# Batch 1's two score groups in joint runs of small matmuls, under a redrawn order of all instructions

## The chip, the cores and the metric

One core of one Trainium2 chip runs the whole kernel. The metric is device time in microseconds (us), the median of three runs. The kernel before took 650.4 us (650.25 to 650.64).

## The reference

A bidirectional attention between 512 tokens `x` and 32 state rows `state` (8 batches, 8 heads, depth 64) feeds a gated two-layer network on all 4,352 rows:

```python
scores = scale * x @ state.T;   xread = softmax(scores) @ state     # tokens read states
scores2 = scale * state @ x.T;  sread = softmax(scores2) @ x        # states read tokens
x = concat([xread, sread]) per batch, heads side by side            # (8*544, 512)
out = (x @ w_a) * (x @ w_b) @ w_out                                 # 512 -> 1536 -> 512, float32
```

## The kernel before, in words

The program is recorded first and emitted later. `attn_moe` calls the engines through `rec`, a recorder; each call becomes a *unit*, and `rec.together()` packs several calls of one engine into one unit that stays in one piece. The 4,904 units are numbered in the order of recording. The string `ORDER` then lists all the numbers in the order in which they are emitted. Each engine works through its own units strictly in that order, so `ORDER` fixes for every engine what stands behind what. Waits between engines follow from the data, and from the reuse of buffers. All DMAs are issued by one queue, SP, also in order; eight DMAs can be under way, and the ninth waits for the first of them to land.

The large products (`layer1`, `layer2`, `term`) are float32r matmuls of 128x128 weights on 512 columns, three for each exact product. Batches 0 and 1 (`WIDE`) get their attention from `Attention`, in two groups `g` of four heads each: `load` (DMA of the tokens `x` and states `st`), `scores` (four small float32 matmuls into a PSUM tile), `scores_t` (ScalarE copies the scores to `kept`, four small matmuls turn them), `soft_t`, `exp`, `norm` (softmax on VectorE and ScalarE), `back_t` (four small matmuls turn the result back; ScalarE copies it as `at_h`, a matmul with `neg` takes that off, ScalarE copies the rest as `at_l`). For batch 0 some more small matmuls that nobody reads stand in the same units (`UNREAD`).

Group 0's `load` writes the tile `x_raw`, of which there is one buffer. For batch 1 its DMA therefore waits until batch 0's group 0 has been read for the last time. Batch 0's readers are its scores and `direct0(f)` for f = 0 and 1: `products` of the states with the freshly joined weights `p_raw` (four conversions from 64-bit numbers, each with a DMA `raw<-wl`, an ACTIVATE `t<-raw`, and two VectorE steps). Group 1's `load` has its own tiles, `xg`.

Units that matter below, as numbered before: batch 0's scores 38 and 52, turns 40 and 54, turn back 48 and 62, `direct0` products 14 and 31, their `neg` matmuls 16, 19, 33, 36; batch 1's loads 112 (`x_raw`) and 127, 128 (`xg`), its scores 113 and 129, turns 115 and 131, turns back 123 and 139; batch 0's first-layer matmuls 80 to 91.

TensorE's units in the order before: 38, 40, 52, 54, 14, 16, 19, 48, 50, 80, 31, 62, 81, 129, 64, 82, 33, 36, 83 and so on, with 131 as 26th, 113 as 33rd, 115 as 39th unit. SP's: 6 (`x_raw` of batch 0), 12 (`xg`), 1 (`raw<-wl`), 13 (`xg`, states), 7, 26, 21 (`raw<-wl`), 66 (`raw<-w_out`), 128, 127, 73, 307, 210, 112.

Of the kernel before, what the change touches and what calls it, by code (L numbers as in the profile page):

```python
# [9 lines left out]
F32 = mybir.dt.float32  # L10
# [9 lines left out]
P = 128  # L20
TOK = S + NS
NG = 2
# [120 lines left out]
6 12 1 13 7 0 26 38-39 21 66 40 128 41-42 3 43 2 44 4 52 45 53 127 9 73 8 46 10 54 14-15 307 55 16 27 56 47 28 18  # L143
57-58 29 19 210 48 59 20 22 49 17 50 23 60 67 80 24 51 61 31 538 62 81 63 32 112 68-69 129 35 64 82 33 65 130 36 83 75
143 546 84 86 74 87 230 562 70 88 76 85 71 89 131 90 92 91 212 96 93 220 34 97-99 113 77 37 94 114 102 172 103 132 175
169 78 231 115 176 95 104 100 133 116 144 105 547 106 177 539 101 134 117 211 118 135-136 173 384 225 119 174 107-108
215 145 109 170 120 166 146 121 137 167 171 122 147 168 110 202 206-207 148 198 194 700 123 195 199 149 308 385 221
138 554 111 124 222 226 386 139 156 125 217 213 140 203 208 710 150 126 379 216 227 196 141 151 157 152 218 555 153
158-159 142 394 540 160 154 197 223 161 556 155 228 244 162-163 711 237 200 178-179 541 245 180 712 181 209 395 182
246 387 396 184 542 247 185 183 186-187 190 374 248 239 188 381 713 204 557 397 249 715 189 389 250 309 191 251 164  # L150
274 720 252 268 380 275 253 205 165 382 254 232 391 558 701 312 269 376 313 255 271 261 256-257 571 375 258-259 277
260 401 278 262 272 377 279 703 280 548 233 201 265 283 730 310 281 549 572 284 273 192 282 390 285 299 392 276 286
193 287 311 543 289 234 288 544 408 300 314 290 302 266 315 722 270 316 706 320 398 317 409 411 235 318 412 321 263
717 322 267 410 264 570 319 323 721 326 402 303 403 714 301 324-325 72 723 612 296 573 5 297 348 327 298 293 342 349
224 79 732 399 350 404 574 343 725 656 559 716 344 351 576 238 352 345 740 346 353 575 616 291 595 294 579 240 593 347
333 354 295 731 545 536 355 304 594 241 563-564 330 419 334 339 420 336 577 560 565 421 335 413 362 578 25 422 242 423
414 393 415 724 596 328 598 292 416 356 340 417-418 424 469 341 733 718 337 614 425 370 338 366 597 735 585 832 441
426 657 470 472 371 331 442 363 332 566 443-444 736 586 604 364 737 550 358 445 726 447 599 471 448-449 365 446 605
587 359-360 741 606 361 615 367 702 567 473 450 617 429 368 451 357 453 329 742 435 430 805 369 372 436 568 734 452
437 842 438-439 719 480 637 440 638-639 618 373 620 431 642 607 432 405 454 481 588 427 463 752 482 466 483 753 306  # L160
474 467 484 727 236 589 640-641 608 475-476 433 621 428 643 477 468 478-479 750 434 457 486 672 458 751 460 464 743
# [5 lines left out]
632 1207 1269 674 1259 524 1260 813 633 1261 525 814 1211 1243 760 1244 1218 1267 1245-1246 1202 761 924 1208 1247 652  # L167
1262 634 1212 1248 635 653 758 553 774 1264 1213 1209 1219 1203 1276 1204 535 388 1226 680 1210 914 775 1250 378 675
776 1448 1214 759 654 764 1222 1383 1270 636 777 1277 676 655 762 517 1418 1271 659 833 765 1272 815 1273 1278 1274
709 763 1279 1275 1227 790 1220 1280 660 1281 771 1282 1284 661 678 1215 662 581 834-835 1285 1283 1223 791 1298 1286  # L170
1290 824 915 1287 677 823 666 1288 1291 1289 1228 1221 1292-1293 219 1294 569 825 1299 1301 1296 1300 1295 1302 1450
1297 687 667 1303 827 663 534 1304 1224 1216 770 780 772 1305 781 773 1309 843 829 1306-1307 1229 778 1217 1310 837
779 1311 830 1312-1314 1308 1331 1315 1385 836 817 1317-1318 664 1332 1316 681 1319-1320 1390 826 1225 1334 1321-1322
1329 1323 682 1324 944 1325-1326 831 844 828 1453 1327 1488 668 1335 1328 1342 816 1451 1333 1330 845 1343 1387 665
1449 1344 1336-1337 1364 793 838 819 1338 582 1339 683 839 1386 1340 1345 1341 820 1230 1452 1346-1347 1388 1348
1350-1352 686 1353-1354 1367 840 1231 1349 1356 792 684 1357 1511 1408 1355 818 1368 1365 788 1358-1360 1362 789 1366
846 1389 926 854 782 821 1361 1454 669 855 1391 916 1363 1369 1470 786 925 1409 688-689 847 1393 1370 927 670 783 1394
935 695 1407 917 936 1371 1395 787 1392 1372 1396 601 1397 852 784 1410 685 1398 1373-1374 853 785 1405 679 690 1417
# [12 lines left out]
1553 1602 1596 1609 1555 1592-1593 1613 1002 888 1603 1617 1558 1621 1604 889 1703 1654 950-951 1160 1635 1605 952
1606 1623 810 1607 1559 1655 981 1608 1610 1636 964-965 903 1614 1556 1004 1618 1161 1641 1619 1009 1696 1637 898 1003
# [3 lines left out]
1784 1694 1722 1658 1661 1168 1684 1669 1664-1665 1700 1666 1686 1689 1755 990 1701 1714 1670 1174 976 1671 1708 1985  # L196
1715 1169 912 1170 1690 1899 1006 1013 1705 1764 1709 1702 1691 1716 1697-1698 1710 1672 1667 1164 1175 1717 1711-1713
1747 1723 1668 1718 1728 1795 1720 1749 1699 1719 1752 1732 1748 1753 1840 1733 1721 1734 1171 1738 1767 1750 1739
1729 1014 1785 1765 1735 1751 1007 1740 1754 1736 1182 1724 1758 1757 1741 1759 1737 1742 1766 906 1783 1988 1761 1744
# [161 lines left out]
def attn_moe(ctx, tc, xt, xn, sd, wl, w_out, out):  # L361
# [238 lines left out]
    class Attention:  # L600
# [29 lines left out]
        def unread(self, k, ps):  # L630
            for _ in range(UNREAD.get((self.b, self.g), (0, 0))[k]):
                nc.tensor.transpose(ps[:, :P], ident, ident)

        def scores_t(self, psp, tag):

            sc = self.raw
# [698 lines left out]
```

## Time and profile before

| | us |
|---|---|
| three timed runs, median | 650.4 |
| the profiled execution, own time | 649.11 |
| its span, first to last instruction | 647.3 |
| TensorE busy | 634.6 (98%) |
| VectorE busy | 560.1 (87%) |
| ScalarE busy | 406.6 (63%) |
| mean granted TensorE clock | 0.995 |

PE is TensorE, DVE VectorE, ACT ScalarE; SPq is the DMA issuing queue. Matmul durations overlap, since matmuls are pipelined: what one costs is the distance from its start to the next start. All units show line 1292, where the recorder emits them; so instructions are told apart by tiles (out<-in).

### The profile page before, as it was taken

The numbers are of one execution on the slowest core, as the hardware profiler recorded it, in microseconds if no ns is written. First come the engines' busy times: TensorE is split into PE (matmuls) and PEld (weight loads), VectorE is DVE, ScalarE is ACT, GpSimd is POOL, SyncE is SP. The second block draws the span as 40 slices with busy tenths as digits, with TensorE's granted clock in tenths as the row PEclk, the third lists the DMA queues.
The fourth block names the chain that finished last, engine by engine and source line by source line (L and its number), as shares of the span: only waits on it lengthen the run. The fifth ranks groups of instructions, "written<-read, shape, count | busy, mean of one in ns | idle before, by whom it ended". The sixth has DMA issues, their size and how long they took to land.

```text
span 647.3 us, 10348 instructions
## 1 busy us (share of the span) xinstructions
PE 634.6 (98%) x3554; PEld 496.5 (77%) x3554; DVE 560.1 (87%) x1037; ACT 406.6 (63%) x753; POOL 0.7 (0%) x6
## 2 busy tenths in 40 slices
PE   7999999999999999999999999999999999999996
PEld 4566777768787888787877877878778888888885
DVE  4899999989779999999999999999967886467885
ACT  4698878699896667557658656743643644345331
POOL 0000000000000000000000000000000000000000
PEclk9899999999999999999999999999999999999999
DMA  8897899999999989999799889998887578658516
GB/s 305 292 379 273 276 328 307 301 359 300 299 322 323 327 311 304 319 329 299 251 283 307 280 314 319 308 286 264 286 228 205 170 173 252 210 154 248 158 34 162
DMA packets 145380, 175.54 MB, mean 271 GB/s; under 512 B 48048, under 2 KB 102832, under 8 KB 145328
## 3 DMA queue, kind: packets, MB, share of 16 engines
q1 hardware_dynamic: 145328, 174.89, 83.4%
q8 instruction: 28, 0.46, 0.3%
q14 instruction: 24, 0.20, 0.1%
HBM read 119.80 MB, written 55.05 MB: 270 GB/s over the span
## 4 chain that ended last, share of the span: by engine, by line
PE 88%; DVE 4%; DMA 3%; ACT 3%; issue 2%; SPq 0%; DVEq 0%; ACTq 0%
PE ab L1292 43%; PE acc L1292 34%; PE ms L1292 11%; DMA xg<-xt 1%; DMA x_in<-f_dram 1%; DVE kept_g L1292 1%; DVE p_l L1292 1%; DMA wt<-wo_dram 1%; ACT p_h L1292 1%; ACT wq L1292 1%; SPq L1292 0%; DMA scr<-sw 0%; DVE p_raw L1292 0%; DVE m L1292 0%; DVE xst L1292 0%
## 5 line engine op out<-in xcount | busy, mean ns | idle before, releaser
L1292 PE MATMUL acc<-g_h,wt 128*128 128x512 f32 x588 | 204.0, 392 | 0.0
L1292 ACT COPY a_sb<-ab 128x512 f32<-128x512 f32 (+1 forms) x120 | 67.8, 566 | 146.3 <-PE ab L1292 131.4
L1292 PE MATMUL ab<-at_h,p_h 128*128 128x512 f32 x384 | 148.1, 396 | 1.7 <-DVE kept_g L1292 1.5
L1292 PE MATMUL ab<-at_l,p_h 128*128 128x512 f32 x384 | 146.3, 392 | 0.0
L1292 PE MATMUL ab<-at_h,p_l 128*128 128x512 f32 x384 | 144.7, 392 | 0.7 <-DVE kept_g L1292 0.6
L1292 PEld LDWEIGHTS acc<-g_h,wt 128*128 128x128 f32 x588 | 109.7, 188 | 25.5 <-issue 1.7
L1292 PE MATMUL acc<-g_l,wt 128*128 128x512 f32 x294 | 108.0, 392 | 0.0
L1292 PEld LDWEIGHTS ab<-at_h,p_h 128*128 128x128 f32 x384 | 72.2, 188 | 25.0 <-ACT a_sb L1292 4.8
L1292 DVE TENSOR_TENSOR g_l<-kept_g,g_h 128x512 fp32r<-128x512 f32 x126 | 84.7, 682 | 5.1 <-PE acc L1292 2.7
L1292 PEld LDWEIGHTS ab<-at_h,p_l 128*128 128x128 f32 x384 | 72.1, 188 | 18.7 <-issue 2.5
L1292 ACT CAST g_h<-kept_g 128x512 fp32r<-128x512 f32 x126 | 75.8, 621 | 16.8 <-DVE kept_g L1292 8.3
L1292 PEld LDWEIGHTS ab<-at_l,p_h 128*128 128x128 f32 x384 | 72.3, 188 | 16.0 <-issue 1.2
L1292 DVE TENSOR_TENSOR kept_g<-ab,a_sb 128x512 f32<-128x512 f32 x84 | 57.5, 685 | 30.8 <-PE ab L1292 17.1
L1292 PEld LDWEIGHTS acc<-g_l,wt 128*128 128x128 f32 x294 | 55.1, 188 | 12.2 <-issue 0.8
L1292 DVE TENSOR_TENSOR stg<-acc,stg 128x512 f32<-128x512 f32 x82 | 55.2, 681 | 8.0 <-PE acc L1292 7.2
L1292 PE MATMUL ab<-xs,sw_st 128*128 128x512 f32 (+1 forms) x192 | 51.4, 338 | 0.5 <-DVE kept_g L1292 0.5
L1292 DVE TENSOR_TENSOR p_l<-p_raw,p_h 128x512 fp32r<-128x512 f32 x72 | 48.7, 681 | 2.0 <-issue 1.8
L1292 ACT CAST p_h<-p_raw 128x512 fp32r<-128x512 f32 x72 | 43.4, 621 | 6.1 <-DMA p_raw<-scr 3.7
L1292 ACT COPY sw<-ms 128x512 f32<-128x512 f32 x72 | 41.7, 586 | 8.8 <-PE ms L1292 8.1
L1292 PEld LDWEIGHTS ab<-xs,sw_st 128*128 128x128 f32 x192 | 34.4, 188 | 7.6 <-DVE kept_g L1292 1.2
L1292 PE MATMUL acc<-g_h,wo 128*128 128x512 f32 x96 | 34.0, 398 | 0.0
L1292 DVE TENSOR_TENSOR kept_g<-kept_g 128x512 f32<-128x512 f32 x42 | 28.6, 680 | 0.1
(128 smaller groups left out, 818.0 us busy)
## 6 DMA issues: line engine op xcount, KB each, us to landing
wt<-s_dram SPq DMA_DIRECT2D x42, 512.0 KB, 6.4
scr<-sw SPq DMA_DIRECT2D x72, 256.0 KB, 5.4
p_raw<-scr SPq DMA_DIRECT2D x36, 512.0 KB, 5.9
wt<-wo_dram SPq DMA_DIRECT2D x63, 256.0 KB, 5.0
raw<-wl SPq DMA_DIRECT2D x24, 512.0 KB, 7.9
x_in<-f_dram SPq DMA_DIRECT2D x36, 256.0 KB, 4.8
out<-turned SPq DMA_DIRECT2D x64, 128.0 KB, 4.4
xn<-xn SPq DMA_DIRECT2D x16, 512.0 KB, 5.9
```

The source lines that it names most:

```text
L1292: getattr(obj, method)(*map(real, args), **{k: real(x) for k, x in kw.items()})
```

## The change

For batch 1, `attend` now loads both groups first, then records both groups' four score matmuls as one unit, both groups' four turns as one unit, and both turns back as one unit. The methods are cut apart for it; batch 0 goes the old way. The unit count falls from 4,904 to 4,901, so every number after the place shifts, and `ORDER` is new from end to end:

```diff
 ORDER = """
-6 12 1 13 7 0 26 38-39 21 66 40 128 41-42 3 43 2 44 4 52 45 53 127 9 73 8 46 10 54 14-15 307 55 16 27 56 47 28 18
-57-58 29 19 210 48 59 20 22 49 17 50 23 60 67 80 24 51 61 31 538 62 81 63 32 112 68-69 129 35 64 82 33 65 130 36 83 75
...
+6 38-39 1 7 12 40-41 2 13 42 9 43-44 3 45-46 21 4 8 47 52-53 10 26 54 48 14 23 0 22 49 24 18 55 28 56 27 29 57 66 15
+31 73 50 58 68 113 19 112 32 59 114 80 60 33 51 61 16 81 67 75 62 17 63 35 82 115 74 116 535 64 117 381 536 83 65 34
...
+        def keep(self):
+            nc.scalar.copy(out=self.raw, in_=self.s)
+            self.s = self.raw
+
         def scores_t(self, psp, tag):
...
+            self.keep()
+            self.turn_in(psp, tag)
+            self.turned()
+
+        def turn_in(self, psp, tag):
             self.t = psp.tile([P, 512], F32, name=tag)
             self.sp = half([P, 16, 32], F32, "s_p")
+
+        def turned(self):
             with rec.together():
                 self.unread(1, self.t)
                 for sb in range(4):
...
+                    nc.tensor.transpose(self.t[:, sb * P:(sb + 1) * P], self.s[:, sb * P:(sb + 1) * P], ident)
...
         def back_t(self, psp, tag):
-            ps = psp.tile([P, 512], F32, name=tag)
+            self.turn_back(psp, tag)
+            self.split()
...
+        elif b:
+            gs = [atts[b, g] for g in range(NG)]
+            for a in gs:
+                a.load()
+            with rec.together():
+                for a in gs:
+                    a.scores(*ms)
+            for a in gs:
+                a.keep()
+            for a in gs:
+                a.turn_in(*ms)
+            with rec.together():
+                for a in gs:
+                    a.turned()
+            for a in gs:
+                a.soft_t()
+                a.exp()
+                a.norm()
+            with rec.together():
+                for a in gs:
+                    a.turn_back(*ms)
+            for a in gs:
+                a.split()
+            return
```

In the numbers of before, the new order of TensorE's units begins: 38, 40, 52, 54, 48, 14, 31, 50, 19, 80, 33, 16, 81, 62, 82, then the joint scores (113 with 129), 64, 83, the joint turns (115 with 131), 36, 86, 87, 84, 85 and so on, with the joint turn back as 45th unit. SP's begins: 6 (`x_raw`), 1 and 7 (`raw<-wl`), 12 and 13 (`xg`), 21 and 26 (`raw<-wl`), 66, 73 (`raw<-w_out`), 127 (`xg` of batch 1), 112 (`x_raw` of batch 1), 128 (`xg`, states, of batch 1). The last ten units or so of TensorE are as before but for small swaps. ScalarE's order begins 39, 2, 43, 8, 53, 0, 22, 49, 18, 27, 57, 15, 32, 51, where 2, 8, 22, 27 are the four conversions, 18, 15, 32 copies of the `direct0` products, and 49, 51 the copies behind batch 0's turn back. VectorE's has the four joins 4, 10, 24, 29 as its 8th, 10th, 12th and 16th units.

## Rows read from the trace of the kernel before

**Rows 1.** The page: each engine's busy time and share of the span.

```profile
PE 634.6 (98%) x3554; PEld 496.5 (77%) x3554; DVE 560.1 (87%) x1037; ACT 406.6 (63%) x753; POOL 0.7 (0%) x6
```

**Rows 2.** Stages (us from the span's start): PE busy, granted clock, DMA share, GB/s.

```profile
20.27:40.00 19.73, 19.73 (x132) 1.00 1.00 362
40.00:640.00 600.00, 597.03 (x3319) 1.00 0.84 270
```

**Rows 3.** Whom TensorE waited for, whole span: us in total, times, longest.

```profile
PE ab L1292 <- DVE kept_g L1292: 2.6, 4, 0.8
PE ab L1292 <- DMA xg<-xt: 1.7, 1, 1.7
```

**Rows 4.** SP's timeline: start, duration, instruction of two loads.

```profile
1.93 0.59 SPq L1292 DMA_DIRECT2D raw<-wl  x1
...
19.11 0.34 SPq L1292 DMA_DIRECT2D x_raw<-xt  x1
```

**Rows 5.** What SP waited for between 11 and 20 us.

```profile
SPq L1292 <- PE acc L1292: 6.5, 1, 6.5
```

**Rows 6.** Loads issued at 1.21, 1.93, 0.74 and 19.11: KB, us to landing.

```profile
xg<-xt SPq DMA_DIRECT2D x1, 512.0 KB, 7.4
raw<-wl SPq DMA_DIRECT2D x1, 512.0 KB, 7.9
x_raw<-xt SPq DMA_DIRECT2D x1, 576.0 KB, 3.5
x_raw<-xt SPq DMA_DIRECT2D x1, 576.0 KB, 4.5
```

**Rows 7.** Timeline, 10 to 19 us, PE, ACT and DVE (wait in brackets).

```profile
10.23 1.06 PE L1292 MATMUL ab<-xg 128*32 128x512 f32 x8 [1.73 <-DMA xg<-xt]
...
11.99 0.66 PE L1292 MATMUL ab<-ident,kept 128*128 128x128 f32 x4
...
13.28 0.37 ACT L1292 CAST p_h<-acc 128x256 fp32r<-128x256 f32 x1 [0.76 <-PE acc L1292]
...
13.30 0.64 PE L1292 MATMUL acc<-p_raw,xg 64*32 64x256 f32 x8
...
13.55 0.67 ACT L1292 ACTIVATE t<-raw 128x512 f32<-128x512 f32 x1
...
17.22 0.69 DVE L1292 SCALAR_TENSOR_TENSOR p_raw<-t,t 128x512 int32<-128x512 int32 x1
...
18.42 0.65 PE L1292 MATMUL acc<-p_raw,xg 64*32 64x256 f32 x4
```

**Rows 8.** Timeline of TensorE around batch 1's scores and turns.

```profile
20.27 1.07 PE L1292 MATMUL ms<-xg 128*32 128x512 f32 x8
21.27 0.50 PE L1292 MATMUL ab<-at_h,neg 128*128 128x512 f32 x1
21.61 0.39 PE L1292 MATMUL ab<-at_h,p_l 128*128 128x512 f32 x1
...
23.94 0.60 PE L1292 MATMUL ms<-ident,kept 128*128 128x128 f32 x4
24.30 0.48 PE L1292 MATMUL ab<-at_l,p_h 128*128 128x512 f32 x1
24.61 0.40 PE L1292 MATMUL ab<-at_h,p_l 128*128 128x512 f32 x1
24.84 0.40 PE L1292 MATMUL ab<-at_h,p_h 128*128 128x512 f32 x1
...
25.86 1.07 PE L1292 MATMUL ms<-x_raw 128*32 128x512 f32 x8
```

**Rows 9.** TensorE in three early stretches: length, busy, granted clock, DMA share.

```profile
8.50:10.20 1.70, 0.00 (x0) 1.00 1.05 413
13.20:16.57 3.37, 1.98 (x17) 1.00 1.06 404
16.57:19.98 3.41, 3.24 (x23) 0.50 0.34 125
```

More of the change, by code (lines that the diff above doesn't have):

```diff
@@ L148 @@
[L148 to L157, printed above, removed]
@@ new lines @@
+2158 2326 2307 2512 2396 2328 2553 2444 1052 2354 2261 2493 2397 2171 2355 2400 2338 2308 2339 2343 2584 1071-1072
+2344 2340 2309 2341 1078 2356 2342 2401 2486 2263 2190 1115 2304 2345 2403 2346 2654 2357 2349 2347 2407 2652
+2416-2417 2404 2348 2440 2402 2374 1069 2408 2418-2419 2577 1082 2358 2350 2305 2188 2360 2376 2436 1091 2441 2405
+2422 2420-2421 2423 2588 2448 1092 2375 2409 2424 2410 2437-2438 2428 2425 2474 2426 1089 2427 2377 2635 2191 2439
+2379 2462 2179 1090 2359 1083 1095 2591 2366 2406 2487 2578 2488 2442 2490 2463 2450 2464 2451 2378 2260 1093 2429
@@ new lines @@
+1084 2491 2579 1102 2367 2456 2492 2494 1957 2465 2262 2181 2496 2385 2449 2470 2386 2517 2513 2489 2534 2514-2515
+2368 2387 2457 2556 2554 2369 1096 2453 2388 2518 2572 2454 2519 2452 2471 2458 2389 2370 2516 1081 2455 1099
+2459-2460 2466 2495 2180 2182 1094 2475 2371 2461 2536 2372 2467 2477 2390 1097 2478 2481-2482 2380 2373 2468 2540
+2585 2391 2498-2499 2469 2361 2500 2504 2392 2140 1109 2505-2506 2544 2507 2501-2502 2586 2541 2159 2497 2535 2476
+2503 2580 2537 2508 2510 2542 2576 2509 599 2581 2511 2520 2538 2521 2483 2522 2433 2523 2543 2526 2545 1110 2524 2527
@@ new lines @@
+2682 2747 2803 2740 2804 2772 2794 2815 2807 2721 2773 1149 2161 2805 2808-2809 1130 2806 2810 2818 2880 2594
+2811-2812 2798 2748 2683 2813 2816 2939 2774 2382 2365 2814 1103 2970 2842 2782 2744 2848 2757 2839 1139 2743 2849
+2775 2783 3039 2843-2845 1108 2846 2784 2850 2742 2841 2776 2684 2795 2851 2827 2847 1140-1141 2741 2785 2957 2854
+1129 2861 2858 2864 2796-2797 2865 2819 2940 2143 2866 2852-2853 2928 2867 2859 2799 2862 2971 2868 1131 2759 2800
+2855 2961 2879 1142 2958 1143 2753 2820 3175 2943 2821 1144 2869 2760 3012 1147 2860 2944 2863 2876 2870-2871 2745
@@ new lines @@
+2685 2872 2822-2823 1138 2925 2960 2972 2922 2926 2973 3080 2873 2824 3183 2945 1148 3013 2941 2927 2874 2975 2923
+1132 2875 2829 2777 2946-2947 2162 2934 2924 2942 2833 2962 3020 3072 2755 2877 2948 2983 2930 2830 1145 2834 2383
+2828 2984 2955 3100 2949 2835 2997 2935 2929 2985-2986 3176 2836 2963 3081 2936 2831 2950 2937 2951 3134 2967 2931
+3017 2987 2968 3021 2969 2980 2676 1154 2988 3083 1146 2832 2932 2952-2953 3018 2976 2954 3019 2959 2761 3135 2253
+2964 3022 3040 2144 2995 2956 2933 3014 3025 2965 2767 2989 2768 3026 2163 3073 1152 2762 2769 3015 3044 3082 3191
@@ new lines @@
+2990 2966 3016 3243 3001 2991 3000 2998 2766 2992 3002 2764-2765 3045-3046 2993 2384 3023 2763 2981 2977-2978 2881
+2994 3041 3061 1153 3042 3084 3003 3024 2882-2883 2996 3027-3028 3043 2982 1151 2979 3194 3029-3030 1156 3037
+3008-3009 3067 3235 3133 3031-3032 2901 3047 3033 3062 3048 2884 3313 2903-2904 2902 3068 3314 3034-3035 3049 3036
+2887-2888 3010 3004 2906 3005 3050 3071 3136 3006 2905 3038 3101 3063 3053 3051 2912 3064 3099 1150 3137 3052 3011
+2889 3278 2885 2890 3054 2999 3108 3069 3077 3055 3065 3059 1155 3078 3070 3158 3085 3066 3180 3007 3086 3346 3181
@@ new lines @@
+2907 2913 3056-3057 3087 3074 3139 3184 3088 3058 3210 3089 3236 3079 2914 3090 3182 3060 3075 3177 3211 3091 3076
+3092 3105 3097 2915 3281 3093 3102 3289 2908-2909 3192 3109 3119 3277 2891 3178 3120 3106 3094-3095 3121 3096 3272
+3188 3122 3179 3103 3123 2916 3185 3107 3140 2886 2910 3284 3124 3285 3098 3376 3193 3196 3195 3357 3189 3156 3197
+3131 3311 3186 3464 3104 3190 3252 3198 3216 3125 3157 3126 3187 3127 3688 3271 3110 2786 3128-3129 3234 3301 3276
+3217 3130 3199 3111 3200 3218 3212 3255 3201 3138 3132 3219 2892 3141 3213 2893 3220 3335 3208 3312 3221 3214 3202
@@ new lines @@
+3337 3215 3315 3273 3115 2894 3416 3116 3203 3112-3113 3222 3204 3114 3316 3318 3244 3117 3237 3205 3465 3360 3206
+3358 3238 3223 3207 3253 3148 3256 3118 3209 3319 2895 3317 3240 3320 3241 3161 3254 3300 3242 3257 2917 3142 2896
+3224 3245 3302 3225 3162 3258 2911 3342 3437 3290 3435 3338 3249 3259 2918 3232 3377 3143 3260 2897 3239 3149 3144
+3261-3262 3226-3227 3481 3228-3229 3343 3163 3269 3398 3246 3250 3230 3417 3263 3282 3145 3286 3345 3159 3441 3264
+3160 3150 3231 3265 3233 3283 3266 3339 3344 3251 3267 3438 3307 3579 3359 3308 3247-3248 3321 3268 3440 3340 3322
@@ new lines @@
+3288 3270 2898 3336 3323 3167 3341 3419 3309 3327 3303 3164 3324 3347 3469 3353 3325-3326 3151 3333 3304 3328 3274
+3361 3329 3466 3454 3330 3168 3305 3310 3331 3443 2899 3275 3354 3348 3332 3477 3334 3349 3306 3362 3152 3363 3381
+3364 3368 3365 3478 3366 3369 3146 2919 3406 3367 3165 3554 3382 3370-3371 3383 3279 3374 3384 3372-3373 3280 3407
+3378 3375 3153 3385 3350 3386 3399 3403 3355 3387 3351 3388 3379 3504 3390 3442 3287 3468 3169 3147 3391 3389 3392
+3482 3166 3393 3470 3444 3380 3291 3396 3394 3352 3404 3395 2900 3421 3677 3527 3405 3170 3412-3413 3400 3446 3356
@@ new lines @@
+3418 3397 3580 3427 3422 3428 3297 3450 3423 3429 3447 3519 3295 3689 3467 3420 3171 3298 3430 3401 3296 3471 3414
+3783 3424 3528 3425-3426 3474 3431 3436 3530 3507 3433 3605 3475 3402 3445 3529 3505 3476 3490-3491 3432 3480 3472
+3492 3408 3473 3434 3415 3483 3520 3748 3172 3624 3409-3410 3496 3714 3531 3497 3411 3484 3493-3494 3448 3625 3495
+3439 3524-3525 3449 3453 3173 3452 3451 3685 3498-3499 3508 3485 3509 3455 3293 3500 3502 3501 3154 3606 3526 3532
+3576 3800 3581 3155 3533 3459 3616 3486 3911 3487 3503 3299 3555 3722 3910 2779 3534 3559 3627 3843 3462 3488 3457
@@ new lines @@
+3521 3878 3174 3461 3538 3522-3523 3626 3539 3463 3535 3686 3292 3560 3536 3540 3537 3460 3541 3458 3548 3803 3479
+3489 3544 3556 3561 3615 3456 3876 3617 3611 3877 3557 3515 3577 3643 3542 3801 3558 3562 3510 3563 3653 3543 3552
+3652 3628 3516-3517 3294 3564 3612 3565 3511 3566 3545 3512-3513 3549 3578 3568 3607 3569 3644 3567 2679 3514
+3546-3547 3613 3550 3570 3792 3574 3608 3971 3678 3518 3571 3582 3572 2781 3583 3573 3584 3575 3621 3553 3622 3585
+3551 3900 3645 3609 3590 2790 2778 3618-3619 3586-3587 3623 3782 3620 2787 3591 3588-3589 3592 3614 3682 3649 3598
@@ new lines @@
+3650 3646-3647 3593-3594 3879 3595 3725 3629 3600 3687 3596-3597 3723 3610 3654 3630 2780 3631 3683 3651 3599 3791
+3632 3601 3648 3690 3684 3506 3679 3635 2788 3655 3741 3633 3680 3634 3636 3641 3637 3749 3840 3638 3602 3639-3640
+3922 3715 3656 3659 3663 3719 2251 3664-3666 3642 3669 4017 3667 2678 3668 3660 3670 3675 3720 3784 3671 3681 4036
+3661 3657-3658 3844 3716 3603 3717 3672 3721 3673 3718 3804 3699 3793 2686 3674 3750 3676 3759 4018 3700 3760 3701
+3691 3702 3692-3695 3742 3901 3726 3751 3696-3698 3703 3819 3704-3705 3724 3707 3785 3706 3662 3708 3710 3727 3761
@@ new lines @@
+4352 3728 3963 3709 3729 4020 3730 3974 3731-3733 3941 3734 3711 3745 3735 3788 3752 3739 3762 3768 3712 3736 3786
+2677 3925 3753 3902 3769 3787 2789 3737 3802 3820 3770 2252 3738 3771 3740 3772 3604 3773 3789-3790 3780 2689 3880
+3805 4037 3806 3774-3775 3807 3794 3923 2254 3776-3779 3883 3869 3821 3808 3743 3845 3809 3841 3781 3881 3795 3811
+3842 3796 3810 3812 4214 3817 3884 3813-3815 4355 3816 3797 3854-3855 3798-3799 3882 3856 3972 2688 3857-3858 3818
+3885 3859 3924 4353 4195 3822 4094 3846 4356 3860 3912 3861 3847 3903 3913 2680 4049 3763 3848 3863 3746 3849 3823
@@ new lines @@
+3850-3851 3865 3852 3904-3906 3754 3853 3892 3831-3832 3893 3862 4052 3907 3824 3886 3825 3887 3747 4040 4128 4041
+3894-3895 4039 3896 3888 3864 3908 3889-3890 3909 3891 4095 4196 3744 3870 3898 3942 3975 3918 3873 4476 3949 4038
+4344 3833 3897 3943 3950 4042 3951 3899 3874 3914 4120 3927 3866 3755 3928 3952 3929 3926 3930 3919 4050 3915
+3953-3954 3961 3713 3834 3931-3932 3944 3920 3871 4198 3933 3946 3875 3939 3934 4154 3955 3964 3973 3935-3936 4186
+3956 3937 4053 3957 3947 3958 4197 3959 3945 4021 4155 3976 3948 3968 3938 4080 3965 3960 3921 3940 3962 3916 4007
@@ new lines @@
+4309 4351 4398 4348 4299 4381 4321 4645 4267 4400 4325 4310-4312 4322 4150 4505 4317 4391 4521 4313-4314 4335
+4315-4316 4417 4318 4336 4247 4337-4338 4550 4339 4392 4428 4418 4340 4790 4399 4264 4358 4342 3757 4394 4478 4393
+4359-4361 4323 4811 4362 4366-4367 4419 4363 4395 4569 4368 4326 4268 4369 4503 4249 4584 4364 4453 4370 4614 4581
+4365 4401 4420 4371 4374 4372 4396 4327 4373 4375 4573 4376 3839 4408-4409 4265 4475 4423 4377 4410 4402 4266
+4403-4404 4324 4405 4411 4406-4407 4412 4250 4424 4328 4434 4269 4425 4413 4585 3826 4414 4437 4506 4431-4432 4415
@@ new lines @@
+3829 4435-4436 4443-4444 4454 4438 4812 4433 4439 4455 4426 4382 4440 4456 4421 4529 4445-4446 4441 4378 4442 4457
+4447 4422 4448 4533 4449 4716 4251 4458 4479-4481 4586 4463 4465 4385 4530 4840 4623 4482 4504 4459 4450 4466 4483
+4487 4574 4610 4386 4531 4534 4484-4485 4532 4488-4489 4634 4490 4460 4552 4535 4491 4736 4572 4486 4673 4555 4737
+4553 4492 3828 4495 4556 4493 4551 4582 4379 4611 4676 4494 4557 4507-4508 4469 3758 4509-4511 4558 4497 4496 4464
+4564 4876 4498 4554 4470 4613 4513 4471 4512 4383 4583 4467 4384 4565 4646 4519 4559-4560 4542 4514 4561 4468
@@ new lines @@
+4757 4767 4770 4758 4762 4846 4803-4804 4785-4786 4831-4832 4847 4608 4848-4849 4793 4701 3827 4805 4794-4795 4627
+4834 4609 4850 4836 4854 4759 4628 4855 4835 4702 4769 4698 4703 4806 4851 4760 4810 4629 4870 4699 4852 4837 4796
+4856 4797 4807 4853 4857 4862 4858 4761 4704 4864 4859-4860 4809 4861 4838 4768 4705 4863 4865 4800 4706 4801 4839
+4866 4871 4799 4872 4771 4877 4873 4878 4874-4875 4879 4867 4884 4808 4885 4868 4886-4887 4798 4880 4889 4881 4888
+4882 4896 4891 4897 4890 4892 4898-4899 4893-4894 4900 4895
@@ L632, in unread @@
                 nc.tensor.transpose(ps[:, :P], ident, ident)
+        def keep(self):
+            nc.scalar.copy(out=self.raw, in_=self.s)
+            self.s = self.raw
         def scores_t(self, psp, tag):
-            sc = self.raw
-            nc.scalar.copy(out=sc, in_=self.s)
-            self.s = sc
+            self.keep()
+            self.turn_in(psp, tag)
+            self.turned()
+        def turn_in(self, psp, tag):
             self.t = psp.tile([P, 512], F32, name=tag)
             self.sp = half([P, 16, 32], F32, "s_p")
+        def turned(self):
             with rec.together():
@@ L654, in back_t, with turn_back @@
         def back_t(self, psp, tag):
-            ps = psp.tile([P, 512], F32, name=tag)
+            self.turn_back(psp, tag)
+            self.split()
+        def turn_back(self, psp, tag):
+            ps = self.ps = psp.tile([P, 512], F32, name=tag)
             sp = self.sp.rearrange("p a b -> p (a b)")
@@ L660, in back_t, with split @@
                                      is_transpose=True, start=(sb == 0), stop=(sb == 3))
-            parts_of(ps, *(t[:, self.g, :] for t in a_t[self.b]))
+        def split(self):
+            parts_of(self.ps, *(t[:, self.g, :] for t in a_t[self.b]))
         def soft(self):
@@ L1001, in attend @@
             if b in WIDE:
-                if b:
-                    a.load()
                 where = ms if b or not g else ab
```

287 lines of the change are left out of this document (111 added, 176 removed), and 22 rows, old and new, of the table ORDER.

## The prediction

> **What bounds the kernel now.** I read the share of busy time first: TensorE is busy 98% of the span [rows 1]. A mean can hide stages, so next the stages: from 20.27 us on TensorE has no idle time up to 40, and 2.97 us in the 600 after that [rows 2]. So from 20.27 us on the kernel is one unbroken string of matmuls, and its end is that start plus the matmuls left plus the few waits. The list of waits says which they are: 2.6 us in four waits for `kept_g`, all after 20 us, and 1.7 us for a load, ahead of 20 us [rows 3]. Everything that this change does is therefore judged by two questions: when does the unbroken string start, and how much work is left then? The DMAs are at full share between 20 and 40 us and at 84% later [rows 2], yet TensorE hardly waits for one, so they stay behind it.
>
> The profiled execution took 649.11 us, 1.8 more than its span, and the three timed runs have a median of 650.4. I work out a difference on the profiled execution and put it on the median.
>
> **What the joint runs save on TensorE.** A group's four score matmuls take 1.00 us from start to start (20.27 to 21.27), and the large matmul after them 0.34 (21.27 to 21.61), where a large matmul among its like takes 0.23 (24.61 to 24.84) [rows 8]: the way out of a small run costs 0.1. The second group's run starts from another large matmul at 25.86 and pays this again [rows 8]. One run of eight pays it once, and drains once; I put the gain at 0.3 us, between 0.1 (the way out alone) and 0.5. The four turns take 0.36 (23.94 to 24.30) and their follower 0.31 [rows 8], together 0.67, and the follower alone would have had 0.23: four turns cost 0.44, or 0.11 each. In a run of four or of eight that is the same, so turns and turns back save nothing; bounds 0 and 0.1 each.
>
> **What the joint runs need.** One score unit now needs both groups' loads. Group 0's load, `x_raw`, has one buffer: in the old order SP sat 6.5 us before it, until the `direct0` products of batch 0 had read it [rows 5], and issued it at 19.11 [rows 4]. It was 4.5 us on its way [rows 6], landing at 23.6. That did not matter: group 1, from other tiles, ran at 20.27, and group 0's scores came only at 25.86 [rows 8]. In the new order the joint scores are TensorE's 16th unit, with nothing of length ahead of them after the products. So the landing of `x_raw` sets the start of the unbroken string. I follow the chain to it.
>
> *The loads.* The old order loaded `xg` second; the new one loads two `raw<-wl` first and `xg` fourth. The second load lands at 1.21 + 7.4 = 8.6, the third at 1.93 + 7.9 = 9.8 [rows 4, 6], so a load of 512 KB lands every 1.2 us. The fourth, now `xg`, lands at 11.0, its 64 KB of states at 11.2. Batch 0's second scores start at 11.3 instead of 10.23 [rows 7]. The two last `raw<-wl` land at 12.4 and 13.6.
>
> *The products.* From scores to turns it was 11.99 - 10.23 = 1.76 us [rows 7], so turns now at 13.1, and 0.5 later the turn back of group 0, which the new order puts ahead of the products: 13.6 to 14.1. The first products take some 0.6 and end (with a last duration of 0.4) at 15.0 (one group: 0.64) [rows 7]. ScalarE's order then has the copy `p_h` (0.37) and only behind it the conversion of the last weights (0.67), VectorE the join (0.69) [rows 7]: 15.0 + 0.4 + 0.7 + 0.7 = 16.8. The last products run from 16.8 to 17.5. In the old order they ended at 18.42 + 0.65 = 19.07 [rows 7]. So `x_raw` is issued at 17.5, 1.6 us earlier than before, with the queues as empty as then.
>
> *The load and the string.* Travelling 4.5 us it lands at 22.0; the first `x_raw` of the kernel needed 3.5 [rows 6], which would be 21.0. I take 4.5, since that load too followed a queue of others. The states of group 1 stand behind it on SP and land some 0.2 later. Until then TensorE has eight short units (50, 19, 80, 33, 16, 81, 62, 82), about 2.0 us with ScalarE's copies between them, done at 19.8. It then idles 2.3 us, and behind the joint scores the whole string waits: 64, 83, the turns, and all the first layer.
>
> *The balance.* The string starts at 22.1, not 20.27: +1.8. By then 33 and 82 are done that were not before, 0.12 and 0.23: -0.35. The joint run: -0.3. Sum **+1.2 us**; with a landing at 21.0 it is +0.1, with products that end 0.5 later (bound: their old end at 19.07 minus 1.0) it is +1.7.
>
> **The clock.** TensorE's clock fell once in the old run: from 16.57 to 19.98 it was granted 0.50, its 1.2 GHz level, after 3.4 us in which TensorE was busy 1.98 us in short pieces. A single pause of 1.7 us at 8.5 left it at 1.00 [rows 9]. That fall was cheap, since TensorE waited for others in it anyway. The new order has two thin places: a pause from 8.3 to 11.3, and the 2.3 us before the joint scores, after short pieces. I expect one fall behind the second, as long as the one on record: 3.4 us at half speed, inside the unbroken string, lose 1.7 us, less some 0.5 where the turns wait for ScalarE's copies anyway: **+1.2 us**. Bounds: 0 (the clock holds) and 3.4 (two falls, both in the string).
>
> **The rest of the order.** Nearly every number of the list has moved, on TensorE by a median of 7 places. What it can give is bounded by the waits there are, -2.9 us [rows 2, 3]; what it can cost is not in the trace, and I take the same size, +2.9. I see no side in the lists: after each tile of the first layer the next user of the same PSUM buffer stands about as far off as before, and the end of the list differs by small swaps. I take 0.
>
> The sum is 1.2 + 1.2 + 0 = +2.4 us, on the median 652.8.
>
> **A rule weighed.** The trace has 4.5 us for `x_raw` in an empty queue, 3.5 at the start [rows 6]. The Trainium skill, "DMA: Bandwidth & Descriptors", section "Anatomy of one DMA", gives a fit for the software path of 2.0 us and the bytes by 436 GB/s, an estimate of 3.4 us here. By that the load would land at 20.9 and the head would cost nothing. No run here times that path, and the row nearest to this case is the 4.5. What the fit would do is the second rival below, priced by the row of 3.5.
>
> **Rivals.**
> *The load comes too late but the clock holds*: +1.2, 651.6. For it: the pause at 8.5 left the clock alone. Against it: that pause came behind an unbroken run, this one behind short pieces.
> *The load comes in time*: it takes 3.5 us as the first one did, lands at 21.0, and the string starts 0.9 after the old one with 0.65 less to do, the clock held: +0.2, 650.6, no difference.
> *Faster: the redrawn list removes the four waits for `kept_g`.* They lie far behind the head, 2.6 us together [rows 3]. A list drawn anew sets the products' users apart in another way, and if all four go, the end comes 2.6 earlier. It decides once the head costs less than that: with the load late and the clock held 650.4 + 1.2 - 2.6 = 649.0; with the load in time 648.0. Against it: a new list makes new close places as it mends old ones.
> *Two falls of the clock*: the pause up to 11.3 is longer than the one that was harmless. If the clock falls there too, the products run at half speed, `x_raw` goes out near 18.6, the string starts near 23.1, with the fall behind it still to pay: 1.2 + 1.0 + 1.6 = +3.8, 654.2.
>
> **How the numbers follow.** The forecast, late load and one fall, has 0.40: 652.8, its own range 651.8 to 653.9. Late load with clock held 0.18: 651.6. Two falls 0.12: 654.2. In time 0.12: 650.6. Waits removed 0.18: 648.0 to 649.0. This kernel's measurement can tell about 0.2% from no change, 1.3 us. Slower by more: the forecast, two falls, and half of the clock-held case, 0.61. Faster by more: 0.17 of the waits removed. The rest, 0.22, is no difference. The range leaves out the lower half of the waits-removed case and the upper part of two falls: 648.9 to 654.6.
>
> **What would show it.** In the new profile: batch 0's second scores at 11.3; the last `direct0` products ending near 17.5; `x_raw` issued there and landing 4 to 4.5 later; a wait of TensorE for `x_raw` of about 2 us, the longest of the list; a second stretch at 0.50 behind it; between 40 and 640 us some 3 us of idle time, as now. The prediction is wrong if the joint scores start before 21 us, if the clock stays at 1.00 behind them, or if the idle time after 40 us has changed by more than 1.5 us.

## The result, and the profile after

| | before | after |
|---|---|---|
| median, four runs each | 650.33 | 654.03 |
| the profiled execution, own time | 649.11 | 654.47 |
| its span | 647.3 | 652.5 |

The ratio is 1.0058, 95% interval 1.0041 to 1.0075: 2.7 to 4.9 us slower. The two profiled executions lie a little further apart than the medians: 5.2 us in the span.

The page of after, busy time and share of the span, answers to [rows 1]:

```profile
PE 637.4 (98%) x3554; PEld 495.9 (76%) x3554; DVE 560.3 (86%) x1037; ACT 406.5 (62%) x753; POOL 0.7 (0%) x6
```

Nothing is to be seen in it. Next the stages of after, as in [rows 2] and [rows 9] (length, PE busy, granted clock, DMA share, GB/s), the last one a stretch of the head:

```profile
20.20:40.00 19.80, 19.80 (x139) 1.00 1.05 385
40.00:640.00 600.00, 594.69 (x3280) 1.00 0.82 266
16.92:20.33 3.41, 3.41 (x15) 0.50 0.77 218
```

The unbroken string starts at 20.20, where it started at 20.27, and there is one stretch at 0.50, as before. But between 40 and 640 us TensorE now idles 5.31 us, not 2.97. One stage of 100 us holds it. Here it is for both kernels (PE, PEld, DVE, ACT, POOL busy, then clock, DMA share, GB/s), first before, then after:

```profile
200.00:300.00 100.00, 99.90 (x460) 79.81 (x459) 95.73 (x166) 66.01 (x119) 0.00 (x0) 1.00 0.96 314
```

```profile
200.00:300.00 100.00, 96.24 (x426) 75.75 (x425) 90.76 (x158) 64.56 (x116) 0.00 (x0) 1.00 0.91 307
```

TensorE lost 3.76 us there, in place of 0.10, and VectorE, which is 96% busy in this stage of before, was busy 5.0 us less. Idle time is not all: a matmul behind a wait also takes longer to its successor (0.34 us from 228.72 to 229.06 in the rows below). Counted from start to start, with 0.227 us for a large matmul among its like and for the small ones their mean in before, TensorE's time over that is 6.2 us in this stage after and 1.1 before, and in all other stages from 20 us on together 15.1 and 14.6. So nearly all of the loss is in this one stage. Whom TensorE waited for in after, the list of [rows 3]:

```profile
PE acc L1327 <- DVE g_l L1327: 2.1, 1, 2.1
PE acc L1327 <- DVE p_raw L1327: 1.9, 2, 1.5
PE ab L1327 <- DMA xg<-xt: 1.5, 1, 1.5
...
PE acc L1327 <- DMA wt<-wo_dram: 0.8, 2, 0.4
```

The waits for `kept_g`, 2.6 us in [rows 3], are gone from it. The longest is new: 2.1 us for one `g_l`. The timelines of TensorE, VectorE, SP and ScalarE tell where it comes from (start, duration, instruction, in brackets the wait before it and what ended it):

```profile
226.21 0.39 PE L1327 MATMUL acc<-g_h,wt 128*128 128x512 f32 x1
228.72 0.50 PE L1327 MATMUL acc<-g_l,wt 128*128 128x512 f32 x1 [2.12 <-DVE g_l L1327]
229.06 0.39 PE L1327 MATMUL ab<-at_l,p_h 128*128 128x512 f32 x1
```

```profile
222.47 0.42 DVE L1327 TENSOR_TENSOR ws<-ws,wf 128x256 f32<-128x256 f32 x1
225.24 0.69 DVE L1327 TENSOR_TENSOR g_l<-kept_g,g_h 128x512 fp32r<-128x512 f32 x1 [2.34 <-DMA s_dram<-ws_h]
226.77 0.69 DVE L1327 TENSOR_TENSOR t2w<-kept_g 128x512 f32<-128x512 f32 x1 [0.84 <-DMA s_dram<-ws_h]
227.38 0.68 DVE L1327 TENSOR_TENSOR kept_g<-kept_g 128x512 f32<-128x512 f32 x1
227.99 0.68 DVE L1327 TENSOR_TENSOR g_l<-kept_g,g_h 128x512 fp32r<-128x512 f32 x1
```

```profile
209.15 0.43 SPq L1327 DMA_DIRECT2D s_dram<-ws_h  x1
...
214.37 0.53 SPq L1327 DMA_DIRECT2D x_in<-f_dram  x1
...
218.27 1.34 SPq L1327 DMA_DIRECT2D s_dram<-ws_h  x2
```

```profile
206.07 0.63 ACT L1327 CAST ws_h<-ws 128x512 fp32r<-128x512 f32 x1
```

`combine` makes `ws_h` and `ws_l`, parts of summed weights, and stores them (`s_dram`). They lie in the pool `lane`, 21 buffers of 128x512 (`half` in the code, `HALF` = 21), which also holds every `g_h`, `g_l`, `a_sb`, `t2w`, `x_in`. VectorE does not wait for data at 222.9 but for a place to write: by the addresses in the built program, the `g_l` of 225.24 stands in the buffer of the `ws_h` that ScalarE wrote at 206.07. That `ws_h` was done at 206.7, but SP issued its store only at 218.27, with another one behind it: SP had sat 2.4 us before the `x_in` of 214.37, which itself needed the buffer of the `ws_h` stored at 209.15. The two stores took 7.5 us on the average and landed at 225.2 and 226.8; the second frees the buffer of `t2w`. The `g_l` that TensorE waits for is the one of 227.99, behind both on VectorE.

The head, as in [rows 4 to 8]: TensorE's timeline, SP's row for `x_raw`, what SP waited for between 10 and 16 us, and the KB and us to landing of that load.

```profile
10.03 1.07 PE L1327 MATMUL ab<-xg 128*32 128x512 f32 x8 [1.54 <-DMA xg<-xt]
...
14.10 0.64 PE L1327 MATMUL acc<-p_raw,x_raw 64*32 64x256 f32 x8 [0.43 <-DVE p_raw L1327]
16.23 0.64 PE L1327 MATMUL acc<-p_raw,xg 64*32 64x256 f32 x8 [1.50 <-DVE p_raw L1327]
...
20.20 1.10 PE L1327 MATMUL ms<-x_raw 128*32 128x512 f32 x8
21.13 1.03 PE L1327 MATMUL ms<-xg 128*32 128x512 f32 x8
22.09 0.50 PE L1327 MATMUL ab<-at_h,neg 128*128 128x512 f32 x1
```

```profile
14.79 0.33 SPq L1327 DMA_DIRECT2D x_raw<-xt  x1
```

```profile
SPq L1327 <- PE acc L1327: 6.4, 1, 6.4
```

```profile
x_raw<-xt SPq DMA_DIRECT2D x1, 576.0 KB, 3.7
```

The second `direct0` unit ran in two halves, group 0's from `x_raw` at 14.10, group 1's from `xg` at 16.23. SP was let go by the first half alone, so the load left at 14.79 and landed at 18.5, 1.7 us before the joint scores. Nothing waited for it.

### The profile page after: what moved, and what is told of

Read it like the earlier page. It is cut to its first block, busy times and chain, and to the rows that moved or that the text cites. A ratio compares the mean times of both kernels' runs of the same rounds, so it can differ in the third digit from the quotient of the medians.

```text
span 652.5 us, 10343 instructions
## 1 busy us (share of the span) xinstructions
PE 637.4 (98%) x3554; PEld 495.9 (76%) x3554; DVE 560.3 (86%) x1037; ACT 406.5 (62%) x753; POOL 0.7 (0%) x6
## 4 chain that ended last, share of the span: by engine, by line
PE 59%; DMA 2%; ACT 2%; DVE 1%; issue 0%; DVEq 0%
PE ab L1327 29%; PE acc L1327 24%; PE ms L1327 6%; DMA wt<-wo_dram 1%; DMA x_in<-f_dram 1%; ACT g_h L1327 1%; ACT wq L1327 0%; ACT a_sb L1327 0%; DVE g_l L1327 0%; DVE xst L1327 0%; ACT p_h L1327 0%; DVE p_l L1327 0%; DVE kept_g L1327 0%; DVE stg L1327 0%; ACT e L1327 0%
## 5 line engine op out<-in xcount | busy, mean ns | idle before, releaser
L1327 PE MATMUL ab<-at_h,p_l 128*128 128x512 f32 x384 | 146.4, 393 | 0.2 <-DVE p_l L1327 0.2
L1327 PE MATMUL ab<-xs,sw_st 128*128 128x512 f32 (+1 forms) x192 | 49.8, 338 | 0.0
L1327 PE MATMUL ms<-wq,sd_h 128*128 128x512 f32 x72 | 28.5, 396 | 0.5 <-ACT sw L1327 0.5
```

Source lines behind the costliest of these rows:

```text
L1327: getattr(obj, method)(*map(real, args), **{k: real(x) for k, x in kw.items()})
```

## Experiments

The theory at this point: the redrawn order costs the time, in one stage, through lane buffers held by late stores; the head and the joint runs cost nothing. The rivals: the head does (late load, half clock); the joint runs do; the loss is spread over the whole list; the transfers are simply saturated near 220 us. Times are medians of the run and of the kernel before on the same chip. The ratio and its interval are worked out from all the runs, so the ratio need not be the quotient of the two medians.

| run | us | before | ratio | 95% interval | span |
|---|---|---|---|---|---|
| e1_joint_old_order | 651.89 | 649.45 | 1.0033 | 1.0017 to 1.0049 | 650.0 |
| e2_apart_new_order | 654.50 | 649.45 | 1.0082 | 1.0058 to 1.0107 | 651.2 |
| e3_new_head_only | 649.85 | 649.45 | 1.0010 | 0.9994 to 1.0026 | 648.3 |
| e4_old_order_195_310 | 659.12 | 649.45 | 1.0145 | 1.0122 to 1.0168 | 657.8 |
| e5_after_again | 653.24 | 650.42 | 1.0053 | 1.0034 to 1.0071 | 651.6 |
| e6_same_queues | 651.46 | 650.42 | 1.0019 | 1.0003 to 1.0035 | 649.0 |
| e7_sp_mended | 650.99 | 650.42 | 1.0015 | 0.9998 to 1.0031 | 649.0 |
| e8_new_till_195 | 648.07 | 650.42 | 0.9971 | 0.9953 to 0.9989 | 646.3 |
| e9_x_raw_read_last | 650.79 | 648.79 | 1.0017 | 0.9999 to 1.0035 | 649.2 |
| e10_apart_best_order | 648.41 | 648.79 | 0.9990 | 0.9977 to 1.0003 | 646.6 |

**The order without the joint runs (e2).** TensorE's units, in the numbers of before:

```diff
-38 40 52 54 14 16 19 48 50 80 31 62 81 129 64 82 33 36 83 ... 131 ... 113 ... 115
+38 40 52 54 48 14 31 50 19 80 33 16 81 62 82 113 129 64 83 115 131 36 86 87 ...
```

> The redrawn order alone: the code of the kernel before with separate units, in the new order, each joint unit replaced by its two parts one behind the other. Theory order: 653.5 to 654.7, as the changed kernel, since the order carries the loss and the joint runs saved 0.3 at most. Rival joint: 649.7 to 651. If the loss is shared, something between.

It is as slow as the changed kernel, and VectorE waits for the same store:

```profile
223.56 0.69 DVE L1292 TENSOR_TENSOR g_l<-kept_g,g_h 128x512 fp32r<-128x512 f32 x1 [1.87 <-DMA s_dram<-ws_h]
```

So the order carries the loss. The separate units, side by side, also take what the joint ones take:

```profile
19.19 1.06 PE L1292 MATMUL ms<-x_raw 128*32 128x512 f32 x8 [0.20 <-DMA x_raw<-xt]
20.07 1.04 PE L1292 MATMUL ms<-xg 128*32 128x512 f32 x8
21.04 0.50 PE L1292 MATMUL ab<-at_h,neg 128*128 128x512 f32 x1
```

21.04 less 19.19 is 1.85 us, where the joint run of after has 1.89 (20.20 to 22.09).

**The joint runs without the order (e1).**

```diff
-... 62 81 129 64 82 33 36 83 ... 131 ... 113 ... 115 ...
+... 62 81 64 82 33 36 83 ... (113 with 129) ... (115 with 131) ...
```

> The joint runs alone: the code of the changed kernel, but the old order of all instructions. A joint run stands where the later of its two parts stood, and the steps of batch 1's group 1 that would come too early stand right behind their counterparts of group 0. Theory order (the redrawn order costs the time, by VectorE waiting between 200 and 300 us for the lane buffers that combine's stores still hold; the joint runs save a few tenths): 649.5 to 650.6, about as before. Rival joint (the joint runs themselves cost, in the softmax of two groups at once or in what stands behind them): 653 to 654.5.

Neither theory's number: 2.1 us over before, by the ratio. All of it is in the head: the matmul that starts at 102.21 in before starts at 104.74 here. Where before has group 1's scores at 20.27 [rows 8], the large matmuls behind them come at once, and the clock stays at half until 23.79, twice as long:

```profile
16.97:23.79 6.82, 5.94 (x31) 0.50 0.70 212
```

The large matmuls run at half speed there. The timed executions say the same: of e1's twelve, the seven with a mean granted clock of 0.991 to 0.994 took 651.8 to 653.2 us, the five with 0.997 to 1.000 took 649.8 to 651.1. Why the clock comes back later the run does not tell. So the joint runs are no gain by themselves: under the old order they cost, under a head drawn for them they don't (e3).

**The head alone, and everything up to 195 us (e3, e8).** Both are the changed kernel, with this edit of the list, K being 217 (about 40 us) and 1445 (about 195 us):

```diff
 ORDER: the first K entries of the new list
-the other entries of the new list
+the same units, in the sequence of the old list
```

> The changed kernel with its own order for the first 40 us, and from there on the remaining instructions in the old order. Theory order: the head was 0.6 to 0.7 us better and the loss lies behind 200 us, so 649.2 to 650.2. Rival head (the loss was made before 40 us, by the second group's scores waiting and the clock at half): 653 to 654.5.

The head is cleared. The span is 1.0 us longer than before's, and one wait where the two orders meet costs more than that:

```profile
PE ab L1327 <- ACT a_sb L1327: 1.8, 2, 1.6
```

> The changed kernel in its new order up to about 195 us and in the old order from there on. If the head is worth 0.65 us, the stretch from 40 to 195 us another 0.3, and the rest costs what it did before: 649.0 to 650.2, 0.0 to 0.2% under the kernel before. Rival head: 653 to 654.5. If the place where the two orders meet costs something, it shows as a single wait near 195 to 205 us.

There is no such wait at this seam, and the stage is as clean as in before:

```profile
200.00:300.00 100.00, 99.90 (x458) 1.00 0.96 312
```

This version beats both kernels: 0.29% under before (0.11 to 0.47), a little better than expected, and 0.82 points under the changed kernel on the same chip (e5). With separate units in the same order (e10) it is 0.10% under before (-0.03 to 0.23), so the size of the gain stays open between about 0.1 and 0.3%; the spans of the profiled executions, 646.3 and 646.6 against 647.3, lie in that range. A part of the 0.29% goes with the clock: its mean over all executions was 0.998 in e8 and 0.995 in before on that chip, where e10 and its before both had 0.997. Whether the new head brought that about is not shown. For e10 0.25 to 0.4% had been expected, more than its interval allows.

**The old order inside the bad stage (e4).**

```diff
 ORDER (new): entries 1 to 1445
-entries 1446 to 2321 (about 195 to 310 us)
+the same units, in the sequence of the old list
 entries 2322 to 4901
```

> The changed kernel in its new order, except that the instructions emitted between about 195 and 310 us stand among themselves as in the old order. Theory order with the loss in 200 to 300 us (3.7 us of idle time there, 0.1 before): 650.0 to 651.0. Rival spread (many small losses all along the list): 652 to 653.5. Rival head: 653 to 654.5.

Every expectation missed: it is the slowest of all. Inside the stretch TensorE idles only 0.72 us:

```profile
200.00:300.00 100.00, 99.28 (x455) 1.00 0.93 306
```

but at its end ScalarE waits 5.4 us for a load that the old sequence issues later than the new one needs it, TensorE waits behind ScalarE, and the clock is at half for 6.8 us after that:

```profile
313.04 1.14 ACT L1327 CAST p_h<-p_raw 128x512 fp32r<-128x512 f32 x2 [5.41 <-DMA p_raw<-scr]
```

The run shows that a sequence decides this stage, and not which; its time can't be used for the size.

**The same queues, other buffers (e6).** The changed kernel again (e5) and a variant in which no engine's own order differs. In the list three ScalarE units, 1854 (`a_sb`), 2043 (`p_h`) and 1189 (`ws_h`), stand further ahead of VectorE's 1879 (`g_l` of 225.24), 1916 (`t2w`), 1857 (the next `g_l`) and others. A tile gets its buffer when its first writer comes up in the list, so only the buffers change hands.

```diff
-1879 1916 1918 1854 1851 1857 1821 2043 1864 ... 1868 1189 1955
+1854 2043 1189 1879 1916 1918 1851 1857 1821 1864 ... 1868 1955
```

> The changed kernel once more, unchanged, as the yardstick for the runs beside it. All theories: 4 to 5 us over the kernel before in the median, with a wait of VectorE of some 2 us near 225 us that ends with a store of combine, and TensorE's longest wait behind it.

> The changed kernel with every engine's own order kept. Only the place of three ScalarE instructions in the common list is moved, ahead of five VectorE instructions near 225 us. That alters nothing but which of the 21 lane buffers each of the next tiles gets: the two buffers whose stores land at 225.2 and 226.8 us now go to ScalarE's tiles, which come late anyway, and VectorE's get buffers that are free. Theory buffers: VectorE's waits of 2.3 and 0.8 us for the stores are gone, TensorE's wait of 2.1 us near 226 with them, and the time falls by 2 to 2.6 us against the changed kernel, to some 651.5. Rival queues (the transfers are saturated there, or the engines' order itself is at fault): no change, within 0.6 us of the changed kernel.

In the yardstick the two waits came as expected, but it lay only 2.8 us over before by the medians and 3.4 by the ratio, not 4 to 5. In e6 the waits for `ws_h` are gone (VectorE's timeline), and with them TensorE's wait of 2.1 us; the stage (second fence) idles 0.79 us:

```profile
222.52 0.43 DVE L1327 TENSOR_TENSOR ws<-ws,wf 128x256 f32<-128x256 f32 x1
222.87 0.69 DVE L1327 TENSOR_TENSOR g_l<-kept_g,g_h 128x512 fp32r<-128x512 f32 x1
223.47 0.68 DVE L1327 TENSOR_TENSOR t2w<-kept_g 128x512 f32<-128x512 f32 x1
224.07 0.68 DVE L1327 TENSOR_TENSOR kept_g<-kept_g 128x512 f32<-128x512 f32 x1
224.67 0.68 DVE L1327 TENSOR_TENSOR g_l<-kept_g,g_h 128x512 fp32r<-128x512 f32 x1
```

```profile
200.00:300.00 100.00, 99.21 (x454) 1.00 0.94 317
```

The ratio falls from 1.0053 to 1.0019, 2.2 us (the spans by 2.6); the mean granted clocks, 0.996 and 0.997, can account for some 0.5 of it. Had saturated transfers or the engines' order as such been at fault here, nothing would have moved: every queue is as it was. So this run shows the cause of the waits near 225 us. It does not account for the whole loss: TensorE's time over that of its matmuls, counted as above, is 2.7 us in this stage, where after has 6.2 and before 1.1, and e6 stays 0.48 points, 3.1 us, over e8, which has the old order behind 195 us.

**SP's order mended (e7).** SP's units, 1169 and 1177 being the two stores of 218.27, 1019 the load `x_in`:

```diff
-1005 1163 1164 808 1019 1816 2042 1825 1792 2111 1169 1177 1012
+1005 1169 1163 1164 808 1816 2042 1825 1177 1792 1019 2111 1012
```

> The changed kernel with three DMAs moved on SP alone near 210 us: two stores of combine issued 8 to 9 us and 2 us earlier, and one load of x_in, which held SP for 2.4 us because it waited for a lane buffer, behind four loads of weights. Theory buffers: no wait for a store near 225 us, and the wait of 0.4 us for the weights near 221 us goes too; 2.6 to 3.4 us less than the changed kernel, to some 651.0. Rival saturated transfers: the stores only push the weights back, TensorE waits for those instead, and at most 1 us is won.

The first store now goes out with that of the other `ws_h`, and `x_in` holds nobody up:

```profile
208.91 1.51 SPq L1327 DMA_DIRECT2D s_dram<-ws_h  x2
...
218.72 0.61 SPq L1327 DMA_DIRECT2D x_in<-f_dram  x1
```

Not all waits are gone: SP now sits 3.0 us before the second store, until ScalarE has written its tile, and VectorE still waits 1.1 us for a store at 214.50; the longest wait of TensorE that its timeline shows between 205 and 229 us is 0.16. The ratio falls to 1.0015, 2.5 us below the changed kernel, a little under the expected 2.6 to 3.4. It ends where e6 ends by another way: the late stores are the cause of this part of the loss, and moved forward they did not push the weights back (TensorE's list of waits has none for `wt`).

**The load as the prediction had it (e9, e10).** On the order of e8, the second `direct0` unit with its halves swapped, so that `x_raw` is read last, and the same order with separate units:

```diff
-                for g in range(NG):
+                for g in (1, 0) if f else (0, 1):
                     self.products(ps[g], f, g, firsts[0, f, g])
```

> The order of the run before (new up to 195 us, old behind it), with the two halves of the second direct0 unit swapped: the group in x_raw is multiplied last instead of first. So the load of batch 1's x_raw can go out only behind the whole unit, near 16.9 us instead of 14.8, as the prediction had assumed for the changed kernel. Theory late load (every part of a us by which x_raw lands late moves the whole string): it lands at 20.6 to 21.4, the joint scores wait for it, start 0.4 to 1.2 us later than 20.2, and the end moves by as much, 648.5 to 649.3 where the same order without the swap had 648.1; with a second stretch at half clock behind the wait up to 1.5 us more. Rival cover (TensorE has other work to the time anyway): no wait for x_raw, no difference.

> The order of the run new up to 195 us, but with the code of the kernel before: batch 1's two groups in units of their own, one behind the other. If what the joint runs give is only that the small matmuls of both groups stand side by side, nothing changes: 647.4 to 648.8, 0.25 to 0.4% under the kernel before, and the sixteen score matmuls take the 1.85 us that the joint run takes. If the joint unit itself saves something: 0.3 us or more above that in the trace.

In e9 SP issues `x_raw` at 17.18, it travels 3.9 us, and the joint scores wait for it; the clock is at half for twice as long (TensorE's timeline, then the stretch):

```profile
15.97 0.65 PE L1327 MATMUL acc<-p_raw,xg 64*32 64x256 f32 x4 [2.56 <-DVE p_raw L1327]
...
21.10 1.55 PE L1327 MATMUL ms<-x_raw 128*32 128x512 f32 x8 [0.51 <-DMA x_raw<-xt]
...
23.44 0.50 PE L1327 MATMUL ab<-at_h,neg 128*128 128x512 f32 x1
...
28.00 1.67 PE L1327 MATMUL ms<-p_raw,six 64*32 64x256 f32 x32 [0.72 <-issue]
```

```profile
15.31:22.14 6.83, 5.65 (x35) 0.50 0.49 135
```

Against e10, on the same chip, that costs 2.4 us by the medians, 1.8 by the ratios and 2.6 by the spans, more than the 0.4 to 1.2 of the late landing alone. Against e8, which differs from e9 by this edit alone but ran on another chip, it is 3.0 by the ratios and 2.9 by the spans. The swap does more than hold the load: both halves of the unit now wait 2.56 us for the last join, where e8 waits 0.43 before the first half and 1.50 before the second. So the run does not tell whether that pause or the late load doubled the stretch at half clock. In e10 the scores run from 20.14 to 21.99:

```profile
20.14 1.06 PE L1292 MATMUL ms<-x_raw 128*32 128x512 f32 x8
21.02 1.04 PE L1292 MATMUL ms<-xg 128*32 128x512 f32 x8
21.99 0.50 PE L1292 MATMUL ab<-at_h,neg 128*128 128x512 f32 x1
...
25.75 1.39 PE L1292 MATMUL ms<-p_raw,six 64*32 64x256 f32 x32
```

1.85 us for units of their own: the joint unit as such saves nothing, standing side by side is all.

## Why the prediction was right, and why it was wrong

The sign and the range held: 3.7 us slower by the medians, 2.4 forecast. The range, 648.9 to 654.6, was wide enough to hold no change too. The reason given for the loss did not hold. The head, put at +2.4, gained about 0.6 (0.1 by the earlier start, 0.34 by units 33 and 82, done before it, 0.2 by the joint runs); the rest of the order, put at 0, lost some 5.8 in the profiled executions (5.2 in the span and the head's 0.6). Two errors covered each other: that the number came near was luck.

*The release of `x_raw`: this step failed.* The prediction let SP go when the last products end, at 17.5. A unit is one piece in its engine's queue, but each of its matmuls ends by itself. The reader of `x_raw` is the first half, which needs only the first of the last two joins; it started at 14.10 and took 0.64. So the load left 2.7 us earlier than worked out; e9, where the same tile is read last, issues it at 17.18, so 2.4 of these come from the release. It also took 3.7 us, not the 4.5 taken from the old `x_raw` of [rows 6]. By the fit in the Trainium skill, "DMA: Bandwidth & Descriptors", section "Anatomy of one DMA", which is for the software path, an estimate is 3.4 us: a landing at 18.2 where 18.5 was measured, nearer than the row chosen. For the 256 KB of a `ws_h` the estimate from the same fit in the Trainium skill is 2.6 us; the two stores of 218.27 took 7.5 on the average, so there the trace does not agree.

*The landings of the head.* Batch 0's second scores came at 10.03, not at 11.3. The second load of the new order took 5.7 us, where the second of the old had 7.4 [rows 6]: I gave a load the travel of another one in its place.

*The late load and the clock: the condition was not met.* In the changed kernel there was no wait before the joint scores and one stretch at 0.50 only. e9 makes the condition true, and pays 1.8 to 3.0 us, where the forecast had +1.2 and +1.2. The sum is near, its parts are not. At the matmul behind the joint scores e9 is 1.45 us later than e10 (23.44 and 21.99). Another 1.1 comes with the small matmuls on `six`, at 28.00 behind a wait of 0.72 for which the trace names nothing (`issue`), a term that the prediction does not have; SP issues the loads behind `x_raw` later in e9 (the next `raw<-wl` at 18.15, in e8 at 15.76), but that this is the reason is not shown. A doubled stretch at 0.50 came, in e9 as in e1, but it began at 15.31, ahead of the wait for `x_raw` and not behind it.

*The joint runs.* Forecast 0.3, bounds 0.1 and 0.5. Measured: both groups' scores take 2.00 us apart (twice 20.27 to 21.27) and 1.89 together, and there is one slow follower of 0.34 in place of two, another 0.1: 0.2. That turns gain nothing was right (eight in 0.79 us, 22.66 to 23.45). e2 and e10 add that units side by side have the same gain.

*The rest of the order: the term that was mis-sized*, 0 with bounds of 2.9 to either side; in the profiled executions the loss was twice the bound. The rival for which the waits for `kept_g` go came true by its condition: they are gone. But one new place cost more than they did. Two things in the old trace spoke for a larger bound and were not read. VectorE's share of 87% [rows 1] was not looked at by stages, and in the stage from 200 to 300 us it is 96%: there, in after, two waits of VectorE of 3.2 us together reached TensorE with 2.1. And of the queues only the order was weighed, not which buffers the tiles that leave by DMA hold until they have landed. The prediction counted how far off "the next user of the same PSUM buffer stands"; the lane's buffers were the ones to count.

Of what would make it wrong, all three came: the joint scores before 21 us, the clock at 1.00 behind them, the idle time after 40 us changed by 2.3.

What stays open: somewhat more than half of what the new order costs behind 195 us. The changed kernel lies 0.82 points, some 5.3 us, over e8; e6 and e7 give back 2.2 and 2.5 of these, and 2.9 to 3.1 are left (2.7 by the spans; the mean granted clocks, 0.997 in e6 and e7 and 0.998 in e8, can account for 0.4). By the count from start to start e6 has 1.2 us more than e8 in the stage from 200 to 300 us (2.7 and 1.5) and 1.3 more in all others (14.8 and 13.5). So the rival of a spread loss holds for this part, as far as the traces tell. Little of it is idle time: e6 idles 2.31 us between 40 and 640 us, e8 2.07. No run took these places one by one.

## What to carry to other kernels

Judge a redrawn list by the tiles that leave by DMA: from the last write to the landing of the store their buffer is taken, and the instruction that gets it next stops its engine's whole queue, whatever its own data. Read the busy share of the second engine in the stage in question, not over the span. And release times go by the last instruction that reads the tile, not by the end of the unit in which it stands.

## What was not expected of the hardware

A store of 256 KB issued near 218 us took 7.5 us in after, where the DMA share is 1.01 (220 to 230 us); one of the same size took 3.5 in before, at 207.6, at a share of 0.94 (200 to 210 us). I had not expected so small a step in the share to go with twice the time; one pair of transfers is no rule.

TensorE's half clock is not bound to a place. Every profiled execution has at least one such stretch ahead of its last matmul, of 3.4 or 6.8 us; where it lies differs even between executions of one kernel. In e5, the changed kernel, the head ran at 1.00 from 5.0 us on (the joint scores started at 18.80, not 20.20), and the clock fell behind the wait of 2.1 us near 225:

```profile
226.87:230.28 3.41, 3.27 (x8) 0.50 0.92 343
```

In the profiled execution of after the same wait left it at 1.00. From the start of the matmul ahead of the wait to that of the same later matmul (226.21 to 259.65 in after, 224.50 to 259.47 in e5) the fall inside the string cost 34.97 less 33.44, 1.5 us.
